# Steps of an attention and Fourier kernel moved between engines and steps: folds, exponentials and the guard of the softmax sums

## The chip, the cores and the metric

The kernel runs on one core of a Trainium2 chip. The metric is the device time of one launch in microseconds, lower is better. A core has five engines that each run their own instructions in order and wait for one another by semaphores: TensorE (PE in the profile; PEld is its weight load), VectorE (DVE), ScalarE (ACT), GpSimd (POOL) and SyncE (SP, which here only issues transfers).

## What is computed

```python
# attention, B=4, H=8, S=768, D=64: 4 sink keys and a window of 128
scores = scale * q @ k.T                       # masked to sink keys and window
a = exp(scores - max(scores))
a = a / (sum(a) + 1e-9)                        # 1e-9: the guard
x = (a @ v)                                    # -> (4, 768, 512)
# Fourier mix and feed-forward
u = x + real(fft(fft(x, axis=1), axis=2))
un = (u - mean(u)) / sqrt(var(u) + 1e-6)
out = u + maximum(un @ w_ch1, 0) @ w_ch2       # 512 -> 2048 -> 512
```

## The kernel before

The four batches are done one after the other, each in six blocks of 128 query rows, 24 blocks in all. A block goes in four steps, one for each pair of heads; `s` counts steps and `k = s % 4`. In every step the program writes out, by the table `SCHEDULE`, what ScalarE ("A"), VectorE ("V"), GpSimd ("G") and TensorE ("T") do, in that order; `SCHEDULE[0]` holds for the first 36 steps (nine blocks), `SCHEDULE[1]` after them. Up to step 97 this order is kept as written; then a scheduler takes over.

The attention of a pair of heads: TensorE makes the scores `s` in PSUM (L702), of which two pairs fit. VectorE merges two key blocks (`merge`, L708) and adds mask and minimum (`soft1`, L720), which frees the scores' place. ScalarE takes the exponentials and their sums (`expo`, L726, two steps later). TensorE turns them (`trans_p`, L751), ScalarE copies the result from PSUM (`copy_p`, tile `pta`, L758), GpSimd cuts it in two by the window (`newer_p` L767, `older_p` L775), and TensorE multiplies by v (`av`, tile `xt`, L789). The four sink keys go their own way: `sink_p` on GpSimd (tile `sk`, L737 and L738), `trans_sink` on TensorE (L809), `copy_sink` on ScalarE (tile `skt`, L814). The turned sink keys lie in the scores' own place of the block two later, so that block's `merge` of its second pair waits for `skt`. Then `copy_x` (L794), `turn_x` and, on VectorE, `store_x` (L819), which multiplies by the inverse of the sums that `inverse` made (L742 adds the guard, L743 takes the reciprocal).

When four blocks of a batch are there, `fourier` sets the batch's Fourier steps in the events "A", "V", "G", "T" and 0 to 3 of later steps, `ready` counting from there. A fold of two blocks (j = 0, 1, 2, four steps apart) is: `fold_n` for the sum on VectorE and the difference on GpSimd (L351), `fold_m` on VectorE (L361) and on GpSimd (L358), `fold_hi` on ScalarE (tile `gh`, L364), `fold_lo` on VectorE (tile `gl`, L367). The middle row of the sequence has its own steps: `put_row`, `mid_sum` (L371) and `mid_row` (tile `sph`: a cast of 33 x 257 at L375, a subtraction of one row at L377). Stage 1 (tiles `za`, `zb`, `zr`, L394) and stage 2 (L421, L442) run on TensorE in the "T" places, and GpSimd adds their results to the blocks (`update`, L458 and L459). The feed-forward network of the first group begins when the attention ends, and overlaps the last batch's Fourier steps and the conversion of the weights (tile `cv`, L590 to L592, on VectorE).

## Time and profile before

| | us |
|---|---|
| median of 3 runs | 787.84 (786.68 to 789.1) |
| the profiled execution, time | 786.78 |
| its span, first to last instruction | 784.9 |
| TensorE busy | 755.2 (96%) |
| VectorE busy | 460.6 (59%) |
| ScalarE busy | 239.0 (30%) |
| GpSimd busy | 177.6 (23%) |

The time of the profiled execution is 1.9 us more than its span: what lies before the first and after the last instruction. Busy shares are over the whole span; the attention takes about the first 220 us of it, and after 262 us TensorE alone is nearly always busy. So the rows below are by stretches of time.

### The profile page before, as it was taken

Reading aid. Unit: us, or ns where it says so; the run is one execution under the profiler, and the core shown is the slowest. Engines: PE = TensorE matmul, PEld = TensorE weight load, DVE = VectorE, ACT = ScalarE, POOL = GpSimd, SP = SyncE. Lnnn points to the kernel's source line nnn. Section 1 sums busy time; section 2 is a strip of 40 time slices with the busy share of each in tenths; the row PEclk is TensorE's granted clock in tenths of the full one; section 3 lists DMA queues with packets and bytes.
Section 4 is the critical chain, followed back from the end, with each engine's and each line's share of the span. In section 5 each row is a group of like instructions: output and inputs, shape, how many; then the busy total and the mean of one; then the engine's idle time right before and its main releaser. Section 6 shows DMA issues by size and latency. Waiting matters only on the chain.

```text
span 784.9 us, 11953 instructions
## 1 busy us (share of the span) xinstructions
PE 755.2 (96%) x4379; PEld 615.8 (78%) x4379; DVE 460.6 (59%) x1354; ACT 239.0 (30%) x704; POOL 177.6 (23%) x283
## 2 busy tenths in 40 slices
PE   7999998988899999999999999999999999999996
PEld 5666876866778878899888888888888888888895
DVE  6788687999999589561356424662456425611211
ACT  4887765756633133221111111111111110110110
POOL 2566477476645255200000000000000000000000
PEclk9999999999999999999999999999999999999999
DMA  9853525433305366120100002000200001000100
GB/s 311 251 171 109 140 84 176 127 112 99 131 27 159 111 196 210 62 71 1 54 1 0 1 9 99 1 1 0 81 1 0 1 0 54 1 1 0 55 1 32
DMA packets 41812, 57.69 MB, mean 74 GB/s; under 512 B 2796, under 2 KB 27500, under 8 KB 41360
## 3 DMA queue, kind: packets, MB, share of 16 engines
q1 hardware_dynamic: 41456, 53.07, 21.7%
q0 software_dynamic: 288, 3.76, 1.2%
q8 instruction: 37, 0.61, 0.3%
q14 instruction: 31, 0.25, 0.1%
HBM read 47.37 MB, written 9.45 MB: 72 GB/s over the span
## 4 chain that ended last, share of the span: by engine, by line
PE 80%; DVE 13%; issue 2%; POOL 1%; ACT 1%; DMA 1%; SPq 0%; DVEq 0%; ACTq 0%; POOLq 0%
PE h L619 33%; PE o L1124 33%; PE xt L789 3%; PE s L702 3%; DVE sm L720 2%; PE pt L751 2%; DVE cv L591 1%; PE za L394 1%; DVE s L708 1%; DVE cv L590 1%; PE a L421 1%; DVE cv L592 1%; DVE f L351 1%; PE x L801 1%; DMA vt<-in_v_sink_dram 1%
## 5 line engine op out<-in xcount | busy, mean ns | idle before, releaser
L1124 PE MATMUL o<-w,h 128*128 128x512 f32 x876 | 216.5, 394 | 0.0
L1117 DVE SCALAR_TENSOR_TENSOR h<-h,h 128x512 fp32r<-128x512 f32 (+1 forms) x107 | 65.4, 611 | 247.7 <-ACT h L1112 247.5
L1124 PEld LDWEIGHTS o<-w,h 128*128 128x128 f32 x876 | 162.8, 188 | 35.5
L1112 ACT ACTIVATE h<-h 128x512 fp32r<-128x512 f32 (+1 forms) x107 | 57.2, 535 | 366.4 <-PE h L619 360.1
L619 PE MATMUL h<-un_slots,w 128*128 128x512 f32 (+1 forms) x576 | 124.7, 365 | 0.0
L619 PEld LDWEIGHTS h<-un_slots,w 128*128 128x128 f32 x576 | 99.6, 188 | 19.6
L619 PE MATMUL h<-un_last,w 128*128 128x512 f32 (+1 forms) x432 | 89.0, 355 | 0.0
L619 PEld LDWEIGHTS h<-un_last,w 128*128 128x128 f32 x432 | 72.7, 188 | 12.8
L726 ACT ACTIVATE sm<-sm,mx 128x132 f32<-128x132 f32 x192 | 75.8, 400 | 7.1 <-DVE mx L720 7.1
L1148 DVE STREAM_TRANSPOSE unf<-un 32x128 f32<-32x128 f32 x224 | 67.7, 302 | 3.2
L702 PE MATMUL s<-ring,q 64*128 64x260 f32 x320 | 51.2, 422 | 12.2 <-DVE mx L720 6.4
L720 DVE CUSTOM_DVE_ANT_0 sm<-s,mask 128x132 f32<-128x132 f32 x192 | 48.7, 292 | 9.3 <-ACT skt L814 2.7
L702 PEld LDWEIGHTS s<-ring,q 64*128 64x128 f32 x320 | 27.1, 188 | 28.2 <-issue 12.4
L608 POOL TENSOR_TENSOR w<-cv,w 128x512 fp32r<-128x512 f32 x25 | 33.9, 1354 | 35.5 <-ACT w L607 35.4
L789 PE MATMUL xt<-ptl,ldv 128*64 128x128 f32 x384 | 38.9, 288 | 0.0
L708 DVE COPY_PREDICATED s<-older,s 128x256 f32<-128x256 uint8 x80 | 33.6, 420 | 7.2 <-ACT skt L814 6.8
L726 ACT ACTIVATION_READ_ACCUMULATOR sm<-sm,mx 128x1 f32 x192 | 36.8, 192 | 0.0
L1124 PE MATMUL o<-w_ring,h 128*128 128x512 f32 x144 | 35.6, 393 | 0.0
L767 POOL TENSOR_SCALAR_AFFINE_SELECT ptl<-pta 128x512 f32<-128x512 f32 x48 | 32.2, 672 | 14.4 <-ACT pta L758 14.4
L789 PEld LDWEIGHTS xt<-ptl,ldv 128*64 128x64 f32 x384 | 21.6, 137 | 14.9 <-issue 8.1
L789 PE MATMUL xt<-pta,ldv 128*64 128x128 f32 x320 | 31.7, 277 | 0.2 <-POOL pta L775 0.2
L751 PE MATMUL pt<-ident,sm 128*128 128x128 f32 x192 | 31.6, 288 | 0.0
(200 smaller groups left out, 1040.9 us busy)
## 6 DMA issues: line engine op xcount, KB each, us to landing
raw<-in_moe_w_ch_dram SPq DMA_DIRECT2D x32, 512.0 KB, 3.7
ldv<-in_v_dram SPq DMA_DIRECT2D x28, 256.0 KB, 3.6
ring<-in_qk_dram SPq DMA_DIRECT2D x24, 264.0 KB, 4.6
out_dram<-u SPq DMA_DIRECT2D x24, 256.0 KB, 3.8
q<-in_qk_dram SPq DMA_DIRECT2D x20, 256.0 KB, 4.2
cst<-in_dft_dram POOLq DMA_DIRECT2D x1, 3348.0 KB, 11.7
ud<-us SPq DMA_DIRECT2D x12, 256.0 KB, 2.2
u<-ud SPq DMA_DIRECT2D x2, 1024.0 KB, 5.1
```

What stands on the lines that cost most here:

```text
L608: G.tensor_tensor(d[1], tf, f32(d[0]), op=ALU.subtract)
L619: T.matmul(ps[:, :tb], a[:, cs], x[:, :, cc, :], start=n == 0, stop=n == 3 * NCC - 1)
L702: T.matmul(ps[:, j, :P + W], st["q", g][rows, hp, :], keys(g, 2 * hp + j), start=True, stop=True)
L708: V.copy_predicated(ps[:, :, P + NS:P + W], older[qi > 2], ps[:, :, 0:P])
L720: V.tensor_tensor_reduce(sm[:, h % 4], ps[:, j, P:P + W], mask[min(qi, 3)], -SCALE, 3.0e38, ALU.add, ALU.min, accum_out=mx[:, 0, h:h + 1])
L726: A.activation(sm[:, h % 4], sm[:, h % 4], AF.Exp, bias=mx[:, 0, h:h + 1], scale=-1.0, accum_out=mx[:, 1, h:h + 1])
L751: T.transpose(ps[:, j], sm[:, j, NS:], ident)
L789: T.matmul(ps[D * j:D * j + D, p, :], st["v", kb(g) - i][:, h, :], a[:, h % 4, :], start=i == 0, stop=i == n - 1)
L1112: A.activation(h[0], ps[:, :tb], AF.Relu)
L1117: V.scalar_tensor_tensor(h[1], ps[:, :tb], 0.0, f32(h[0]), op0=ALU.max, op1=ALU.subtract)
L1124: T.matmul(po[i], a[:, ts_], x, start=f == 0 and n == 0, stop=f == NF - 1 and n == 2)
L1148: V.transpose(unf[32 * q:32 * q + 32, :, r], un[r].rearrange("p (c q j) -> p c q j", c=NCC, q=4)[:, :, q])
```

## The change

Three things are edited. The steps of a fold get other places: `F_STEPS[1]` for j = 0 and 1, `F_STEPS[0]` for the last j and the last batch; GpSimd's `fold_n` comes one step later, its `fold_m`, `fold_hi` and `fold_lo` one step later where j is 0 or 1. The middle row's cast goes from VectorE to ScalarE (`mid_hi`), and its subtraction (`mid_lo`) three steps later. The adding of the guard goes from VectorE to GpSimd as a step of its own (`floor`), and the reciprocal one step later. In ScalarE's lists the exponentials come ahead of the copies in two of the four steps of `SCHEDULE[0]` and one of `SCHEDULE[1]`.

```diff
-F_N, F_M, F_S, ROW = (3, 3), (4, 5), (6, 7), (5, 8, 10)
+F_STEPS = ((3, 4), (4, 5), (6, 7)), ((3, 4), (4, 6), (7, 8))
+ROW = 5, 8, 9, 13
...
-    "inverse": 7,
+    "floor": 6,
+    "inverse": 8,
...
         "A": [
             ["copy_x", "copy_p", "copy_sink", "expo", "A", "sink_hi"],
-            ["copy_x", "copy_sink", "expo", "sink_hi", "A", "copy_p"],
+            ["copy_x", "expo", "copy_sink", "copy_p", "A", "sink_hi"],
             ["copy_x", "copy_p", "copy_sink", "expo", "A", "sink_hi"],
-            ["copy_x", "A", "copy_p", "copy_sink", "expo", "sink_hi"],
+            ["expo", "copy_x", "A", "copy_p", "copy_sink", "sink_hi"],
...
-            ["copy_x", "copy_sink", "A", "sink_hi", "copy_p", "expo"],
+            ["copy_x", "expo", "copy_sink", "copy_p", "A", "sink_hi"],
...
         "G": [
...
-            ["newer_p", "older_p", "sink_p", "G"],
+            ["newer_p", "older_p", "sink_p", "floor", "G"],
...
-                def mid_row():
+                def mid_hi():
+                    A.copy(sph[:NR, :257], t_["x0"][:, :257])
+
+                def mid_lo():
                     t = t_["x0"]
-                    V.tensor_copy(sph[:NR, :257], t[:, :257])
                     lo = sph[NR - 1:NR, :257]
                     V.tensor_tensor(lo, t[NR - 1:NR, :257], f32(lo), op=ALU.subtract)
...
+                    f_n, f_m, f_s = F_STEPS[0 if tail or j == NHALF - 1 else 1]
...
-                at(ready[0] + ROW[2], "V", mid_row)
+                at(ready[0] + ROW[2], "A", mid_hi)
+                at(ready[0] + ROW[3], "V", mid_lo)
...
                     def inverse(g):
                         mx = st["mx", g]
-                        V.tensor_scalar_add(mx[:, 2], mx[:, 1], 1e-9)
                         V.reciprocal(mx[:, 2], mx[:, 2])
+
+                    def floor(g):
+                        mx = st["mx", g]
+                        G.tensor_scalar_add(mx[:, 2], mx[:, 1], 1e-9)
```

What stands where, in the program's order. Line numbers of the change are some lines higher. First VectorE in the second batch, between the last `soft1` of a block (its accumulator is the first row) and the first `merge` of the next, where the fold j = 2 begins. Before:

```order
L720 ISA mx_1658 128x1
L742 TENSOR_SCALAR mx_1512<-mx_1512 128x8
L743 RECIPROCAL mx_1512<-mx_1512 128x8
L375 CAST sph<-xr_1440 33x257
L377 TENSOR_TENSOR sph<-xr_1440,sph 1x257
L367 TENSOR_TENSOR gl_1429<-f_1_1_1654,gh_1428 128x512
L351 TENSOR_TENSOR f_1_2_1778<-us_2_1072,us_5_1075 128x512
L708 COPY_PREDICATED s_0_1769<-older_122,s_0_1769 128x2x128
```

And with the change, the same place and the one two merges later:

```order
L727 ISA mx_1657 128x1
L749 RECIPROCAL mx_1512<-mx_1512 128x8
L354 TENSOR_TENSOR f_1_2_1776<-us_2_1069,us_5_1072 128x512
L715 COPY_PREDICATED s_0_1766<-older_122,s_0_1766 128x2x128
...
L727 ISA mx_1780 128x1
L370 TENSOR_TENSOR gl_1429<-f_1_1_1653,gh_1428 128x512
L364 TENSOR_TENSOR f_1_2_1776<-f_1_2_1776 128x255
L829 TENSOR_TENSOR u_65<-x_1801,mx_1385 128x512
L382 TENSOR_TENSOR sph<-xr_1440,sph 1x257
L715 COPY_PREDICATED s_2_1825<-older_122,s_2_1825 128x2x128
```

Of six instructions between two pairs' scores two are left; `gl` and the subtraction for `sph` now stand two pairs later, and the guard and the cast have left VectorE.

Second GpSimd in the same batch, from the cut of one block (`ptl_1`) to that of the next pair (`ptl_3`). Before:

```order
L767 AFFINE_SELECT ptl_1_1730<-pta_1_1694 128x512
L775 AFFINE_SELECT pta_1_1694<-pta_1_1694 128x512
L358 TENSOR_TENSOR f_1_1_1654<-f_1_1_1663 128x255
L737 CAST sk_1761<-sm_0_1657 128x2x16
L738 TENSOR_TENSOR sk_1761<-sm_0_1657,sk_1761 128x2x16
L458 TENSOR_TENSOR u_64<-u_64,d_1_1650 128x257
L459 TENSOR_TENSOR u_64<-u_64,d_1_1650 128x255
L767 AFFINE_SELECT ptl_3_1785<-pta_3_1751 128x512
L351 TENSOR_TENSOR f_1_2_1787<-us_2_1072,us_5_1075 128x512
L775 AFFINE_SELECT pta_3_1751<-pta_3_1751 128x512
```

And with the change:

```order
L777 AFFINE_SELECT ptl_1_1731<-pta_1_1691 128x512
L785 AFFINE_SELECT pta_1_1691<-pta_1_1691 128x512
L753 TENSOR_SCALAR mx_1512<-mx_1512 128x8
L744 CAST sk_1757<-sm_0_1656 128x2x16
L745 TENSOR_TENSOR sk_1757<-sm_0_1656,sk_1757 128x2x16
L463 TENSOR_TENSOR u_64<-u_64,d_1_1650 128x257
L464 TENSOR_TENSOR u_64<-u_64,d_1_1650 128x255
L361 TENSOR_TENSOR f_1_1_1653<-f_1_1_1704 128x255
L777 AFFINE_SELECT ptl_3_1783<-pta_3_1752 128x512
L785 AFFINE_SELECT pta_3_1752<-pta_3_1752 128x512
```

The guard is new behind the cut; GpSimd's half of `fold_m`, which completes the tile that `gh` is cast from, now stands behind `sk` and an update; and its half of `fold_n` no longer stands between the two cuts of a pair.

Third ScalarE around the same cast `gh`. Before:

```order
L758 COPY pta_3_1751<-pt_3_1738 128x512
L364 CAST gh_1428<-f_1_1_1654 128x512
L726 ACTIVATE sm_2_1727,mx_1658<-sm_2_1727,mx_1658 128x132 x2
L814 CAST skt_1811<-s_1_1772 128x128
L758 COPY pta_1_1813<-pt_1_1799 128x512
L726 ACTIVATE sm_2_1727,mx_1658<-sm_2_1727,mx_1658 128x132 x2
```

And with the change:

```order
L768 COPY pta_3_1752<-pt_3_1739 128x512
L367 CAST gh_1428<-f_1_1_1653 128x512
L733 ACTIVATE sm_2_1728,mx_1657<-sm_2_1728,mx_1657 128x132 x4
L824 CAST skt_1809<-s_1_1769 128x128
L768 COPY pta_1_1811<-pt_1_1795 128x512
```

The cast `gh` stands at the same place; the exponentials of the block's last pair have moved from behind `pta` to ahead of `skt`, and both now follow `gh`.

## Rows read from the trace of the kernel before

**Rows 1.** Windows: length, busy of PE, PEld, DVE, ACT, POOL; PEclk, DMA.
```profile
48.00:70.00 22.00, 19.96 (x178) 13.27 (x178) 20.30 (x86) 18.16 (x70) 16.80 (x32) 1.00 0.33 97
70.00:98.00 28.00, 28.00 (x259) 23.30 (x257) 17.90 (x78) 19.14 (x71) 12.53 (x26) 1.00 0.52 147
98.00:125.00 27.00, 23.01 (x193) 17.49 (x189) 23.06 (x81) 15.98 (x60) 20.95 (x37) 0.94 0.22 61
140.00:186.00 46.00, 39.70 (x357) 30.39 (x358) 44.63 (x164) 28.90 (x103) 30.22 (x52) 1.00 0.35 103
200.00:262.00 62.00, 56.91 (x350) 48.38 (x347) 58.72 (x100) 24.08 (x56) 34.05 (x31) 0.97 0.34 107
```

**Rows 2.** Timeline of VectorE: start, duration, line, operation.
```profile
115.00 0.65 DVE L375 CAST sph<-xr 33x257 fp32r<-33x257 f32 x1
115.69 0.74 DVE L377 TENSOR_TENSOR sph<-xr,sph 1x257 fp32r<-1x257 f32 x1
116.46 1.01 DVE L367 TENSOR_TENSOR gl<-f,gh 128x512 fp32r<-128x512 f32 x1
117.39 1.76 DVE L351 TENSOR_TENSOR f<-us,us 128x512 f32<-128x512 f32 x1
```

**Rows 3.** Timeline of TensorE, the wait in brackets.
```profile
120.19 0.71 PE L702 MATMUL s<-ring,q 64*128 64x260 f32 x4 [2.31 <-DVE mx L720]
```

**Rows 4.** Windows of 4 us where TensorE's clock was lower, columns as rows 1.
```profile
121.00:125.00 4.00, 3.92 (x26) 2.72 (x26) 2.88 (x14) 1.23 (x5) 3.77 (x9) 0.57 0.02 1
210.00:214.00 4.00, 4.00 (x18) 3.58 (x16) 4.00 (x9) 1.53 (x3) 1.66 (x2) 0.57 0.53 170
```

**Rows 5.** Windows of line L742 alone, the guard: busy and count.
```profile
48.00:70.00 22.00, 0.83 (x4) 1.00 0.33 97
98.00:125.00 27.00, 1.11 (x3) 0.94 0.22 61
140.00:186.00 46.00, 1.11 (x5) 1.00 0.35 103
200.00:262.00 62.00, 1.08 (x2) 0.97 0.34 107
```

**Rows 6.** Windows of line L375 alone, the cast of the middle row.
```profile
48.00:70.00 22.00, 0.23 (x1) 1.00 0.33 97
98.00:125.00 27.00, 0.65 (x1) 0.94 0.22 61
140.00:186.00 46.00, 0.56 (x1) 1.00 0.35 103
200.00:262.00 62.00, 0.72 (x1) 0.97 0.34 107
```

**Rows 7.** Line L737, GpSimd's small cast: count, ns minimum/median/maximum.
```profile
L737 POOL CAST sk<-sm x48: 205/212/500, 10.6 to 206.1; 128x32 fp32r<-128x32 f32 x48
```

**Rows 8.** Timeline of GpSimd beside rows 2.
```profile
113.61 0.73 POOL L358 TENSOR_TENSOR f<-f 128x255 f32<-128x255 f32 x1
...
114.78 0.73 POOL L458 TENSOR_TENSOR u<-u,d 128x257 f32<-128x257 f32 x1
115.46 0.69 POOL L459 TENSOR_TENSOR u<-u,d 128x255 f32<-128x255 f32 x1
...
116.90 1.70 POOL L351 TENSOR_TENSOR f<-us,us 128x512 f32<-128x512 f32 x1
```

**Rows 9.** Timeline of ScalarE beside rows 2.
```profile
114.37 0.62 ACT L364 CAST gh<-f 128x512 fp32r<-128x512 f32 x1
...
117.25 0.27 ACT L814 CAST skt<-s 128x128 fp32r<-128x128 f32 x1 [1.47 <-PE s L809]
```

**Rows 10.** Waits, 0 to 225 us: total, times, longest.
```profile
ACT skt L814 <- PE s L809: 24.4, 18, 2.7
...
DVE s L708 <- ACT skt L814: 6.8, 11, 1.3
```

**Rows 11.** Line L726, an exponential: count, ns minimum/median/maximum.
```profile
L726 ACT ACTIVATE sm<-sm,mx x192: 387/399/427, 5.9 to 205.5; 128x132 f32<-128x132 f32 x192
```

**Rows 12.** Line L351, the fold's first step: ns minimum/median/maximum by form.
```profile
L351 DVE TENSOR_TENSOR f<-us,us x9: 639/693/1758, 95.8 to 228.6; 128x512 f32<-128x512 f32 x9
```

More of the change, by code (lines that the diff above doesn't have):

```diff
@@ L99 @@
             ["newer_p", "older_p", "G", "sink_p"],
-            ["newer_p", "G", "sink_p", "older_p"],
+            ["newer_p", "G", "sink_p", "older_p", "floor"],
             ["newer_p", "older_p", "sink_p", "G"],
@@ L466, in fourier @@
                     k = ready[j]
+                    f_n, f_m, f_s = F_STEPS[0 if tail or j == NHALF - 1 else 1]
                     e0, e1 = FOLD_TAIL if tail else FOLD_ENG
                     eng = {"V": V, "G": G}
-                    at(k + F_N[0], e0, lambda j=j: fold_n(eng[e0], j, 0))
-                    at(k + F_N[1], e1, lambda j=j: fold_n(eng[e1], j, 1))
-                    at(k + F_M[0], e0, lambda j=j: fold_m(eng[e0], j, 0))
-                    at(k + F_M[1], e1, lambda j=j: fold_m(eng[e1], j, 1))
-                    at(k + F_S[0], "A", lambda j=j: fold_hi(j))
-                    at(k + F_S[1], "V", lambda j=j: fold_lo(j))
+                    at(k + f_n[0], e0, lambda j=j: fold_n(eng[e0], j, 0))
+                    at(k + f_n[1], e1, lambda j=j: fold_n(eng[e1], j, 1))
+                    at(k + f_m[0], e0, lambda j=j: fold_m(eng[e0], j, 0))
+                    at(k + f_m[1], e1, lambda j=j: fold_m(eng[e1], j, 1))
+                    at(k + f_s[0], "A", lambda j=j: fold_hi(j))
+                    at(k + f_s[1], "V", lambda j=j: fold_lo(j))
                 at(ready[0] + ROW[0], "V", put_row)
                 at(ready[0] + ROW[1], "V", mid_sum)
-                at(ready[0] + ROW[2], "V", mid_row)
+                at(ready[0] + ROW[2], "A", mid_hi)
+                at(ready[0] + ROW[3], "V", mid_lo)
                 k = ready[2] + S1
@@ L951, in window_attention @@
                             "newer_p": newer_p, "older_p": older_p, "av": av, "copy_x": copy_x, "copy_sink": copy_sink,
-                            "trans_sink": trans_sink, "turn_x": turn_x, "inverse": inverse, "store_x": store_x,
+                            "trans_sink": trans_sink, "turn_x": turn_x, "inverse": inverse, "floor": floor, "store_x": store_x,
                             "sink_hi": lambda g: g and g % NB == 0 and sink_hi(g // NB), "sink_lo": lambda g: g and g % NB == 0 and sink_lo(g // NB),
```

## The prediction

> **What bounds the kernel now.** I read the windows by stretch first, since the busy shares of the whole span mix two kernels: behind 262 us TensorE is never short of work and the change touches nothing there. Before that the stretches are of two kinds [rows 1]. From 70 to 98 us TensorE is busy for all 28.00 us, and whatever VectorE saves there buys nothing (125 to 140 and 186 to 200 us are of this kind too). Where the folds of a batch lie, TensorE waits: 22.00 - 19.96 = 2.04 us from 48 to 70, 3.99 us from 98 to 125, 6.30 us from 140 to 186, and 5.09 us from 200 to 262. In these four VectorE is busy for 20.30 of 22, 23.06 of 27, 44.63 of 46 and 58.72 of 62 us. So 17.4 us of TensorE's waiting are all that this change can win directly, and VectorE is what it has to win them from.
>
> Then I read VectorE's timeline at the longest of these waits, in the second batch. Four instructions of the fold stand in a row between two pairs of scores: the middle row's cast, its subtraction, `gl`, and the sum of the next fold, from 115.00 to about 119.1 us [rows 2]. The scores that TensorE has to make next lie behind them, and it waits 2.31 us, released by VectorE [rows 3]. After that wait its granted clock is 0.57 on average for 4 us, which is the lower level of 1.2 GHz for most of them [rows 4]. A second window like it stands at 210 us.
>
> **The change, part by part.** The guard leaves VectorE 24 times. Only those in the four stretches count: 0.83, 1.11, 1.11 and 1.08 us of busy time, 14 instructions in all [rows 5]. From the end of one such instruction to the next some 0.03 us pass (the same that separates 115.69 + 0.74 from 116.46 in [rows 2]), so 14 x 0.03 = 0.4 us come on top. One of the four in the first stretch stands ahead of a VectorE wait, so I take off 0.2 us. That makes 4.13 + 0.4 - 0.2 = 4.3 us.
>
> The cast of the middle row leaves VectorE four times, once in each stretch: 0.23 + 0.65 + 0.56 + 0.72 = 2.16 us [rows 6], with 0.03 us each 2.3 us.
>
> By stretch the two make 1.0, 1.9, 1.85 and 1.9 us, each well below TensorE's waiting there, so I count all of it: 6.6 us.
>
> The steps that move (`gl`, the fold's first sum, the subtraction of the row, GpSimd's halves) are the same instructions as before. Their total is credited with nothing. What the move can give is in where they stand: the row of four in [rows 2] becomes one, and `gl` and the subtraction come two pairs later, beside `fold_m` and `store_x`. The wait of 2.31 us should then break into shorter ones, and shorter waits have not brought the clock down: the whole of 140 to 186 us, with 6.30 us of waits, was granted 1.00 [rows 1]. The drop at 121 us cost (1 - 0.57) x 4 = 1.7 us of TensorE's work [rows 4]; VectorE was busy for 2.88 of those 4 us, so 1.1 us of it was time in which VectorE, too, had nothing to do. I credit 1.1 us, with bounds of 0 (the wait only moves) and 3.4 us (both drops go, at their full 1.7 us). The one at 210 us stands in the scheduler's part, where the order of the conversions changes in ways that I can't price; I leave it in.
>
> Now what is added. GpSimd's guard has no row. The nearest is its cast of a 128 x 32 tile, 205 ns at least, 212 in the median and 500 at most [rows 7]; a tile of 128 x 8 is smaller, so 0.2 us, 24 x 0.2 = 4.8 us of GpSimd's time. It stands behind the second cut of the block's first half, and the reciprocal comes two steps later. GpSimd is free for 5.2 of 22, 6.05 of 27 and 15.8 of 46 us in the fold stretches [rows 1], so nobody should wait for the result. What can cost is that the two engines disturb each other: the fold's sum took 1.76 us where GpSimd's own half (116.90, 1.70 us long) was running [rows 2, 8], against 639 ns at least [rows 12]. VectorE's instruction ended 0.5 to 0.6 us after GpSimd's, as if it had begun only then. So the bounds for 24 more GpSimd instructions are 0 and 24 x 0.2 = 4.8 us, and since most of VectorE's instructions here (merges, soft1) read PSUM and show no such rows, I take a tenth, 0.5 us. A gain is possible as well, since the cast no longer runs on VectorE; it is within this.
>
> The Trainium skill's page "SBUF — State Buffer" (section "Who interferes with whom") says it as a rule: a VectorE instruction with two SBUF inputs and a GpSimd instruction that reads SBUF take the shared read port as a whole, and whichever comes second stands still. The rows agree (0.64 against 1.76 us). By that rule the guard on GpSimd is a new holder of the port and speaks against the change, up to the 4.8 us of the bound, and the fold's halves may meet anew in their new places; that is the second rival below.
>
> ScalarE's order. In the steady blocks an exponential pair takes 2 x 0.39 us [rows 11] and moves into time in which ScalarE waited anyway: 24.4 us over 18 waits for the sink keys' transposition, 1.36 us each [rows 10]. I price it at 0; without that cover it would hold `skt` back by up to 0.78 us a block, and VectorE already waits 6.8 us for `skt` [rows 10].
>
> One wait is added. `gh` needs GpSimd's half of `fold_m`, which before stood ahead of the sink cast (113.61) and now stands behind it and behind an update of 0.73 + 0.69 us [rows 8]. `gh` itself stays at its place behind `pta`, at 114.37 in the old trace [rows 9]. Three folds have an update in front in this way (both early ones of the second batch and one of the third, by the order). Behind a late `gh` stand both exponential pairs of the block's second half and `skt`, and behind `skt` VectorE's merge. GpSimd's work in front is 1.42 us longer, ScalarE had 1.47 us of slack ahead of `skt` there [rows 9], and the merge is itself to come earlier by what VectorE saves. Bounds 0 and 3 x 1.42 = 4.3 us; I take half, 2.1 us. The middle row's cast on ScalarE is at most the 0.62 us of `gh` [rows 9], four times, and lies in the same waits: 0.
>
> **The sum.** 4.3 + 2.3 + 1.1 - 0.5 - 2.1 = 5.1 us. 786.78 - 5.1 = 781.7 us for an execution like the profiled one. The median of the runs is 1.06 us above that execution, so I forecast 782.8 us (-0.65%).
>
> **Rivals.**
> 1. *More than the sum.* If the row of four was the cause of most of TensorE's waits in the stretches, half of the 17.4 us go and both clock drops with them: 8.7 + 3.4 = 12 us, 775.8. For it: VectorE's contended instructions stand in that row (1.01 and 1.76 us [rows 2]). Against it: VectorE is busy 85 to 97% of these stretches [rows 1], and what moves is not removed.
> 2. *Given back by the port.* `gl` and `fold_m` now stand where GpSimd does its half of `fold_n`. A fold's instruction that meets it grows by 1.76 - 0.64 = 1.1 us [rows 2, 12]. With the six early folds of three batches meeting it at half that more than before, 3.4 us are lost, and with 0.5 of the sum's other costs doubled the gain is about 1.2 us: 786.6, no change. For it: GpSimd is busy 76 to 78% of the first two stretches [rows 1]. Against it: before, GpSimd's half met the same engine's sum just as often.
> 3. *Slower: ScalarE stands still at `gh`.* In the three places the exponentials, `skt` and the next merge all queue behind it. If `gh` is late by 1.9 us (1.42 and a sink cast of 0.5), VectorE and then TensorE wait as long, and a wait of about 2 us brings TensorE's clock down for another 1.7 us [rows 3, 4]. 3 x (1.9 + 1.7) = 10.8 us against the 7.2 us of the sum without its 2.1: 3.6 us slower, 791.4. It decides where the late `gh` exceeds ScalarE's slack ahead of `skt`, 1.47 us [rows 9], by more than VectorE comes earlier. Against it: the merge has no wait in that place in the old trace.
>
> The change does what it says by the order, so that it does nothing is no rival of its own; that VectorE's savings end in TensorE-bound time is part of rival 2's outcome.
>
> **How the numbers follow.** Chances: the sum 0.55, rival 1 0.10, rival 2 0.21, rival 3 0.14. The forecast's own range is 778 to 786. 0.3% of 787.84 is 2.4 us, about what a measurement of this kernel can tell from no change, so faster is below 785.5 and slower above 790.2. Faster takes rival 1 and nearly all of the sum, 0.64; same takes rival 2 and the sum's upper end, 0.23; slower is 0.13. The range leaves out the far half of rival 1 and most of rival 3: 777 to 789.
>
> **What would show it.** Right: line L742's successor stands on GpSimd at 0.1 to 0.3 us; VectorE's busy time falls by at least 6 us (4.1 of guard in the four stretches and 2.2 of cast, more or less by contention); TensorE's waits in the four stretches fall by about 5 us, above all in 98 to 125 us; no 2 us wait near 120 us, and the clock there is 1.00. Wrong: ScalarE idle ahead of `gh` until GpSimd's `fold_m` for over 1 us, with VectorE waiting for `skt` behind it (rival 3); VectorE's `gl` at 1.0 us or more beside GpSimd's `fold_n` (rival 2); VectorE waiting for GpSimd ahead of the reciprocal, which I exclude. The forecast would also be wrong if the order of the conversions behind step 97 moves TensorE's waits after 200 us by more than 2 us either way.

## The result: 0.27% slower, and the profile after

The changed kernel takes 789.07 us in the median of 20 runs (787.37 to 793.2), the kernel before beside it 787.14 us (785.75 to 789.1). The ratio is 1.0027 with a 95% interval of 1.0016 to 1.0037. So it is 2 us slower where I forecast 5 us faster. The profiled execution took 788.54 us, its span is 786.8 us.

The first view is the windows by stretch, against [rows 1]: length, then busy time of PE, PEld, DVE, ACT, POOL, then the granted clock. The last row, 44 to 262 us, holds all folds; ahead of it the guard and ScalarE's new order act as well.

```profile
48.00:70.00 22.00, 20.03 (x172) 13.60 (x170) 17.32 (x74) 16.83 (x65) 17.45 (x31) 0.92 0.31 86
70.00:98.00 28.00, 26.44 (x238) 21.51 (x236) 17.28 (x74) 18.18 (x66) 12.81 (x29) 1.00 0.51 147
98.00:125.00 27.00, 23.90 (x220) 18.61 (x218) 19.48 (x80) 18.05 (x69) 19.92 (x34) 1.00 0.25 70
140.00:186.00 46.00, 40.55 (x356) 32.04 (x354) 40.56 (x165) 30.45 (x111) 30.95 (x56) 1.00 0.39 114
200.00:262.00 62.00, 56.27 (x363) 48.44 (x362) 59.52 (x106) 26.24 (x64) 38.53 (x35) 1.00 0.35 115
44.00:262.00 218.00, 198.60 (x1610) 159.18 (x1609) 180.03 (x588) 130.31 (x451) 142.22 (x227) 0.98 0.39 120
```

The same stretch, 44 to 262 us, in the kernel before:

```profile
44.00:262.00 218.00, 200.42 (x1600) 159.93 (x1601) 190.68 (x607) 129.66 (x446) 132.10 (x210) 0.98 0.39 119
```

VectorE is lighter by more than I said: 17.32 in place of 20.30 us, 19.48 in place of 23.06, 40.56 in place of 44.63 (but 59.52 in place of 58.72 in the last stretch). From 44 to 262 us it is busy for 180.0 us, before for 190.7. Yet TensorE's idle time there went up, from 218 - 200.42 = 17.6 to 218 - 198.60 = 19.4 us. The next view shows VectorE's waits from 44 to 262 us (total, times, longest).

```profile
DVE s L715 <- ACT skt L824: 14.7, 13, 2.5
DVE sm L727 <- ACT skt L824: 3.2, 2, 1.9
```

In the same stretch of the kernel before:

```profile
DVE s L708 <- ACT skt L814: 3.9, 7, 1.3
DVE sm L720 <- ACT skt L814: 2.7, 2, 1.6
```

VectorE waits 17.9 us for `skt`, before it was 6.6 us. So over the whole change a longer wait for `skt` stands against the 10.7 us that were taken off VectorE. The experiments below show that the two don't come from the same parts.

The first batch's fold is the best place to see where the time goes. First VectorE's timeline (start, duration, line, operation, the wait in brackets). L370 is `gl` (before L367), L364 `fold_m`, L374 the middle row's sum, L829 `store_x`, L715 a merge.

```profile
58.18 0.43 DVE L715 COPY_PREDICATED s<-older,s 128x256 f32<-128x256 uint8 x1 [0.78 <-ACT skt L824]
...
59.08 1.08 DVE L370 TENSOR_TENSOR gl<-f,gh 128x512 fp32r<-128x512 f32 x1
60.08 0.85 DVE L364 TENSOR_TENSOR f<-f 128x255 f32<-128x255 f32 x1
60.85 0.41 DVE L374 TENSOR_TENSOR xr<-xr 33x255 f32<-33x255 f32 x1
61.19 0.67 DVE L829 TENSOR_TENSOR u<-x,mx 128x512 f32<-128x512 f32 x1
61.79 0.41 DVE L715 COPY_PREDICATED s<-older,s 128x256 f32<-128x256 uint8 x1
...
67.76 0.43 DVE L715 COPY_PREDICATED s<-older,s 128x256 f32<-128x256 uint8 x1 [2.54 <-ACT skt L824]
```

The row of four of [rows 2] is gone, and another row of four stands here, 2.7 us long, between the second and the third pair of scores. Beside it, ScalarE's timeline: L377 is the middle row's cast, L367 `gh`.

```profile
61.29 0.41 ACT L377 CAST sph<-xr 33x257 fp32r<-33x257 f32 x1 [1.60 <-DVE xr L374]
...
63.81 0.62 ACT L367 CAST gh<-f 128x512 fp32r<-128x512 f32 x1 [0.38 <-POOL f L361]
...
120.57 0.62 ACT L367 CAST gh<-f 128x512 fp32r<-128x512 f32 x1 [2.16 <-POOL f L361]
```

The cast waits for the row's sum, with a pair of exponentials right behind it, and at 120.57 `gh` waits 2.16 us for GpSimd, as rival 3 has it. TensorE's timeline shows the price of the row (eight score matmuls in one line), and the windows below it the clock. The profile names no releaser for this wait ("issue"); that the row sets it follows from the times, since the pair's `soft1` behind the merge of 61.79 us ends at 62.74 us.

```profile
62.85 2.18 PE L709 MATMUL s<-ring,q 64*128 64x260 f32 x8 [1.66 <-issue]
```

```profile
61.00:65.00 4.00, 2.34 (x12) 0.94 (x10) 3.90 (x18) 3.33 (x11) 2.32 (x6) 0.76 0.52 133
65.00:69.00 4.00, 3.85 (x33) 3.05 (x33) 1.43 (x9) 2.53 (x13) 2.81 (x6) 0.82 0.00 0
184.00:188.00 4.00, 2.49 (x14) 1.48 (x16) 4.00 (x15) 2.75 (x11) 3.93 (x6) 0.74 0.39 128
188.00:192.00 4.00, 4.00 (x33) 3.59 (x30) 2.56 (x12) 1.53 (x6) 2.46 (x5) 0.83 0.50 170
```

The low clock of [rows 4], at 121 and 210 us, is gone: both windows are at 1.00 in this execution. Two others have come, near 64 and 187 us, and they cost the same: (0.24 + 0.18) x 4 = 1.7 us, and 1.7 us again.

### The profile page after: what moved, and what is told of

Its sections match the earlier page's. It is cut to its first block, busy times and chain, and to the rows that moved or that the text cites. A ratio compares the mean times of both kernels' runs of the same rounds, so it can differ in the third digit from the quotient of the medians.

```text
span 786.8 us, 11950 instructions
## 1 busy us (share of the span) xinstructions
PE 754.0 (96%) x4379; PEld 616.1 (78%) x4379; DVE 450.2 (57%) x1326; ACT 239.7 (30%) x708; POOL 189.6 (24%) x307
## 4 chain that ended last, share of the span: by engine, by line
PE 78%; DVE 13%; DMA 3%; issue 3%; ACT 2%; POOL 1%; SPq 0%; DVEq 0%; ACTq 0%; POOLq 0%
PE o L1134 32%; PE h L626 32%; PE xt L799 3%; PE s L709 3%; DMA ring<-in_qk_dram 3%; DVE cv L598 2%; PE pt L761 2%; DVE sm L727 1%; PE za L399 1%; ACT sm L733 1%; DVE s L715 1%; DVE cv L597 1%; DVE cv L599 1%; PE a L426 1%; PE x L811 1%
## 5 line engine op out<-in xcount | busy, mean ns | idle before, releaser
L615 POOL TENSOR_TENSOR w<-cv,w 128x512 fp32r<-128x512 f32 x25 | 36.7, 1469 | 33.9 <-ACT w L614 33.7
L715 DVE COPY_PREDICATED s<-older,s 128x256 f32<-128x256 uint8 x80 | 33.8, 422 | 18.7 <-ACT skt L824 17.5
L777 POOL TENSOR_SCALAR_AFFINE_SELECT ptl<-pta 128x512 f32<-128x512 f32 x48 | 33.8, 705 | 32.6 <-ACT pta L768 30.2
L768 ACT COPY pta<-pt 128x512 f32<-128x512 f32 x48 | 28.1, 585 | 10.4 <-PE pt L761 10.2
```

The source lines that it names most:

```text
L615: G.tensor_tensor(d[1], tf, f32(d[0]), op=ALU.subtract)
L715: V.copy_predicated(ps[:, :, P + NS:P + W], older[qi > 2], ps[:, :, 0:P])
L777: G.affine_select(lo, a, [[0, 4], [s, P]], compare_op=ALU.is_ge, fill=0.0, base=0, channel_multiplier=-s)
```

## The experiments

Eighteen kernels were timed, each against the kernel before on the same chip. Three theories stood at first: ScalarE stands still at its two late casts (A), VectorE and GpSimd get in each other's way (B), and, after the first runs, VectorE's pile has only moved (C). The table lists all results; behind the ratio stand four readings of each profile. *Idle* is 218 us less TensorE's busy time from 44 to 262 us, *clock* the sum of (1 - granted clock) x 4 us over the windows of 4 us from 40 to 264 us, *VectorE* its busy time and *skt* its wait for `skt`, both from 44 to 262 us. These four are of the profiled execution alone, which need not be like the median one: e9's took 788.36 us with a median of 784.76, e17's 787.03 with 785.30, e10's 783.31 with 785.00.

| kernel | ratio to before (95%) | idle | clock | VectorE | skt |
|---|---|---|---|---|---|
| before | 1 | 17.6 | 3.4 | 190.7 | 6.6 |
| after | 1.0027 (1.0016 to 1.0037) | 19.4 | 3.4 | 180.0 | 17.9 |
| e1 row's cast at 10 | 1.0051 (1.0039 to 1.0063) | 19.2 | 5.2 | 180.5 | 15.7 |
| e2 GpSimd's `fold_m` at 5 | 1.0061 (1.0044 to 1.0078) | 18.5 | 6.8 | 178.6 | 16.8 |
| e3 both | 1.0059 (1.0039 to 1.0080) | 20.8 | 3.4 | 181.1 | 16.6 |
| e4 old fold steps | 1.0006 (0.9990 to 1.0022) | 17.4 | 1.7 | 185.4 | 10.5 |
| e5 `gl` at 10 | 0.9974 (0.9964 to 0.9984) | 16.2 | 3.4 | 182.4 | 11.1 |
| e6 guard alone | 0.9968 (0.9958 to 0.9978) | 17.4 | 0.0 | 185.6 | 6.5 |
| e7 cast alone | 0.9966 (0.9954 to 0.9978) | 16.3 | 1.7 | 188.6 | 7.0 |
| e8 order alone | 1.0055 (1.0042 to 1.0068) | 19.4 | 3.4 | 192.3 | 7.1 |
| e9 old order, `gl` at 10 | 0.9972 (0.9963 to 0.9980) | 17.8 | 6.8 | 179.9 | 13.7 |
| e10 guard and cast | 0.9975 (0.9963 to 0.9987) | 17.8 | 0.0 | 184.5 | 7.8 |
| e11 old order | 1.0001 (0.9991 to 1.0010) | 19.2 | 5.2 | 180.1 | 13.4 |
| e12 order, GpSimd's sum at 4 | 1.0074 (1.0061 to 1.0087) | 17.8 | 5.1 | 189.5 | 7.7 |
| e13 guard twice | 1.0041 (1.0019 to 1.0063) | 20.1 | 3.4 | 193.8 | 7.2 |
| e14 fold behind first pair | 0.9995 (0.9978 to 1.0012) | 19.0 | 1.7 | 183.2 | 8.0 |
| e15 order, third pair | 1.0032 (1.0018 to 1.0046) | 20.1 | 1.7 | 193.0 | 6.4 |
| e16 order, first pair | 1.0036 (1.0023 to 1.0049) | 18.5 | 3.4 | 190.6 | 8.6 |
| e17 guard and cast, cast at 10 | 0.9967 (0.9954 to 0.9980) | 18.4 | 3.4 | 184.8 | 7.8 |
| e18 guard, cast, late order | 0.9986 (0.9971 to 1.0001) | 17.3 | 0.0 | 185.0 | 8.1 |

The mean granted clock of every execution was measured too, and it varies within one kernel: from 0.987 to 0.997 in the 113 executions of the kernel before, from 0.992 to 0.998 in the eleven of e10. An estimate of what the clock costs, at the most, is (1 - clock) x span; it is too high where TensorE waits at the low clock. Its mean is 5.2 us in the 29 executions of the kernel before that ran beside e10 and e11, 3.2 us in e10 and 6.0 us in e11; 5.8 us in e8 with 5.6 us beside it; 8.5 us in e13 with 4.9 us beside it.

### Are ScalarE's late casts the cause?

These four are edits of the changed kernel. e1:

```diff
-ROW = 5, 8, 9, 13
+ROW = 5, 8, 10, 13
```

> The changed kernel with one number different: ScalarE's cast of the middle row one step later (10 in place of 9), behind the next pair of exponentials. Theory A (ScalarE stands still at the two casts that wait): the cast waited 1.60 us at 61.3, 1.05 at 116.3, 2.10 at 171.6 and 1.05 at 225.9 for VectorE's sum of that row, with exponentials behind it; these waits fall below 0.3 us each, the exponentials and the sink cast come earlier, and of the 2.9 us that the first batch's folds lost about 1.5 come back, of the third batch about 1: 2 to 3 us less than the changed kernel, 786 to 787, ratio to the kernel before 0.999 to 1.000. Theory B (the cost is contention of VectorE with GpSimd at gl and the fold's sums): the same instructions stand in the same order on VectorE, so nothing is won, ratio 1.002 to 1.004.

e2, and e3 with both this edit and that of e1:

```diff
-F_STEPS = ((3, 4), (4, 5), (6, 7)), ((3, 4), (4, 6), (7, 8))
+F_STEPS = ((3, 4), (4, 5), (6, 7)), ((3, 4), (4, 5), (7, 8))
```

> The changed kernel with GpSimd's half of fold_m of the first two folds back at step 5 (as before the change; all else as changed). Theory A: gh waited for it 2.16 us at 120.6 and 0.92 at 127.9; at step 5 it stands in front of the sink cast and of the update, in a time where GpSimd was idle for 1.5 us, gh begins at once behind pta, and VectorE's wait of 2.09 us for skt at 122.9 goes: 1.5 to 2.5 us less than the changed kernel, about 787, ratio 0.999 to 1.001. Theory B: fold_m on GpSimd moves away from VectorE's next fold sum (1.23 us in place of 0.72), half a microsecond per fold at most, at most 1 us: 1.001 to 1.003.

> The changed kernel with both edits: the middle row's cast at step 10, and GpSimd's half of fold_m at step 5. Theory A: the two gains stand in different steps and add, 3.5 to 5.5 us less than the changed kernel: 783.5 to 785.5, ratio 0.995 to 0.998, which is about what the prediction's sum without its term for the late gh comes to (5.1 + 2.1 = 7.2 us less than before), less the loss near 33 us. Theory B: at most 1 us less than the changed kernel, ratio 1.001 to 1.003.

e4:

```diff
-F_STEPS = ((3, 4), (4, 5), (6, 7)), ((3, 4), (4, 6), (7, 8))
+F_STEPS = ((3, 3), (4, 5), (6, 7)), ((3, 3), (4, 5), (6, 7))
```

> The changed kernel with the fold's steps of before on all engines (first sums at 3, fold_m at 4 and 5, gh at 6, gl at 7); guard, row's cast and ScalarE's order stay as changed. Theory A: gl no longer stands in front of fold_m and of the row's sum, so the cast at step 9 waits 1.0 us less than in the changed kernel, and gh waits no more for GpSimd; the row of four is then one of three on VectorE, since the row's cast is gone from it, and a wait of TensorE of 1 to 1.5 us is back near 120 us: in all 1 to 3 us less than the changed kernel, 786 to 788, ratio 0.999 to 1.001. Theory B: the old places of the fold had less contention: 3 us or more less than the changed kernel, ratio below 0.998.

Theory A fell. In e1 the cast waits for VectorE's sum 0.9 us once, in place of 5.8 us in four places; in e2 `gh` waits for GpSimd 0.8 us once, in place of 3.7 us in four; in e3 both are short. None became faster, all three are slower than the changed kernel. VectorE's timeline in e1 shows why taking the wait away won nothing.

```profile
59.75 0.69 DVE L370 TENSOR_TENSOR gl<-f,gh 128x512 fp32r<-128x512 f32 x1
60.36 0.85 DVE L364 TENSOR_TENSOR f<-f 128x255 f32<-128x255 f32 x1
61.13 0.84 DVE L374 TENSOR_TENSOR xr<-xr 33x255 f32<-33x255 f32 x1
61.90 0.68 DVE L829 TENSOR_TENSOR u<-x,mx 128x512 f32<-128x512 f32 x1
62.50 0.41 DVE L715 COPY_PREDICATED s<-older,s 128x256 f32<-128x256 uint8 x1
```

TensorE's timeline in e1, at the same place:

```profile
63.57 0.71 PE L709 MATMUL s<-ring,q 64*128 64x260 f32 x4 [1.66 <-issue]
```

The row of four is still there, the merge behind it comes at 62.50, and TensorE waits the same 1.66 us. With the old fold steps (e4) that row has no `gl` in it, VectorE waits 10.5 us for `skt` and not 17.9, and 1.0006 against 1.0027 brings back 1.7 us (the intervals overlap). That e1 to e3 are slower than the changed kernel and not equal to it goes for e1 and e2 with the clock column, for e3 with the idle one; which wait brings the clock down I could not foresee in any of them.

### One part at a time

e5 is the changed kernel with `gl` in the other gap; e6 to e8 are the kernel before with one part each (the fold's steps alone were not run).

e5:

```diff
-F_STEPS = ((3, 4), (4, 5), (6, 7)), ((3, 4), (4, 6), (7, 8))
+F_STEPS = ((3, 4), (4, 5), (6, 7)), ((3, 4), (4, 6), (7, 10))
```

> The changed kernel with gl of the first two folds at step 10 in place of 8, so that it stands behind the reciprocal, in the other of VectorE's two gaps between pairs of scores. The two earlier theories were the waits of ScalarE (A) and contention (B); the waits could be taken away without a gain. Theory C (the pile moved): the change put gl in front of fold_m, the row's sum and store_x, a new row of four of 2.7 to 3.1 us between two pairs of scores (59.75 to 62.50 with the row's cast late), while the other gap holds 0.9 us and VectorE then waits 1.1 to 2.5 us for skt. With gl there the gaps are 2.0 and 1.6 us, TensorE's waits of 1.8 and 1.5 us near 63 and 72 us fall below 1.0 each, VectorE's wait for skt falls by half from its 13 us, and the time is 1.5 to 3 us below the changed kernel: 786 to 787.5, ratio 0.998 to 1.001. Theory A: gh and the row's cast wait as before this edit, 789, ratio 1.002 to 1.004. Theory B: gl meets GpSimd's first sum of the next fold less or more, within 1 us of the changed kernel, 1.001 to 1.004.

e6, with `floor` as in the change:

```diff
-    "inverse": 7,
+    "floor": 6,
+    "inverse": 8,
...
-                        V.tensor_scalar_add(mx[:, 2], mx[:, 1], 1e-9)
```

> The kernel before with one part of the change alone: the guard on GpSimd behind the second cut, and the reciprocal a step later; the rest as before. The prediction's terms: -4.3 + 0.5, 3.8 us less than before, ratio 0.995. Theory C: the guard takes 0.2 us out of one of the two gaps, but which pair TensorE waits for is decided by the longer gap and by skt, so most of it turns into VectorE's wait for skt (6.8 us in the kernel before): 0 to 1.5 us less, ratio 0.998 to 1.000. Theory B: the guard disturbs VectorE by up to 4.8 us: 1.000 to 1.006.

e7, with the steps 9 and 13:

```diff
-                    V.tensor_copy(sph[:NR, :257], t[:, :257])
+                    A.copy(sph[:NR, :257], t_["x0"][:, :257])
```

> The kernel before with the row's cast alone on ScalarE (step 9) and its subtraction at step 13. The prediction's terms: -2.3 us, and the part of the clock drop at 121 us that hung on the row of four (-1.1): ratio 0.996 to 0.997. Theory C: the gap with gl, the row's cast and its subtraction is the longer one in the kernel before (2.3 us against 1.8 near 60 us), so that taking cast and subtraction out of it is worth more than the guard: 1 to 3 us less, and the wait of 2.31 us near 120 us falls below 1.5, ratio 0.996 to 0.999. Theory A: the cast waits for the row's sum and holds ScalarE up by about 1 us in each of four batches: 1.001 to 1.004.

e8, which takes the new "A" rows of the change and nothing else (here the first of them):

```diff
-            ["copy_x", "copy_sink", "expo", "sink_hi", "A", "copy_p"],
+            ["copy_x", "expo", "copy_sink", "copy_p", "A", "sink_hi"],
...
```

> The kernel before with ScalarE's new order alone (exponentials ahead of the copies that wait). The prediction: 0 us, ratio 1.000. From the traces: the second cut on GpSimd then begins at the moment at which VectorE makes two small products near 33.4 us, which grew from 0.21 and 0.26 to 0.62 and 0.69 us, once, 0.8 us in all; theory C expects no more than that, ratio 1.000 to 1.002. If the order were what holds skt back in each block (0.39 to 0.78 us a block, as the prediction bounded it), 24 blocks would cost 5 us and more: ratio above 1.005.

In VectorE's timeline of e5 the row is one of three (and TensorE's wait behind it 1.11 us):

```profile
60.10 0.76 DVE L364 TENSOR_TENSOR f<-f 128x255 f32<-128x255 f32 x1
60.79 0.84 DVE L374 TENSOR_TENSOR xr<-xr 33x255 f32<-33x255 f32 x1
61.56 0.67 DVE L829 TENSOR_TENSOR u<-x,mx 128x512 f32<-128x512 f32 x1
...
64.04 0.69 DVE L370 TENSOR_TENSOR gl<-f,gh 128x512 fp32r<-128x512 f32 x1
```

One number, `gl` from step 8 to 10, is worth 1.0027 - 0.9974 = 0.0053, 4.2 us. That is theory C in kind and more than its range, though TensorE's wait fell to 1.11 us and not below 1.0. With ScalarE's old order the same number is worth 2.3 us (e9 below against e11).

Guard and cast alone give 2.5 and 2.7 us. For the cast that is within the prediction's range and theory C's; for the guard it lies between the prediction's 3.8 us and theory C's 1.5 at the most. In e6 TensorE's idle time falls from 12.5 to 10.3 us between 44 and 200 us, as the prediction has it, and rises from 5.1 to 7.1 us from 200 to 262 us, most of which the scheduler orders. One of the waits there is for GpSimd's second cut: it is 1.4 us or more in every kernel with the guard on GpSimd, and 0.2 us or none in the others. TensorE's waits from 200 to 262 us, in the kernel before and the changed one:

```profile
PE xt L789 <- POOL pta L775: 0.2, 1, 0.2
PE xt L799 <- POOL pta L785: 1.5, 2, 1.1
```

With the guard the scheduler also orders GpSimd's other work anew there, so what the guard itself does to this wait isn't told apart.

ScalarE's order, which I had priced at nothing, costs 4.3 us alone. That is the total expected if it held `skt` back in every block, but VectorE's wait for `skt` is 7.1 us, against 6.6 before. VectorE's timeline in e8, at the second fold of the first batch (`gl` and the fold's sum):

```profile
56.90 1.02 DVE L369 TENSOR_TENSOR gl<-f,gh 128x512 fp32r<-128x512 f32 x1
57.84 1.76 DVE L353 TENSOR_TENSOR f<-u 128x512 f32<-128x512 f32 x1
```

GpSimd's timeline there, its half of the same fold:

```profile
57.35 1.71 POOL L353 TENSOR_TENSOR f<-u 128x512 f32<-128x512 f32 x1
```

TensorE's timeline behind it:

```profile
60.65 0.71 PE L705 MATMUL s<-ring,q 64*128 64x260 f32 x4 [1.20 <-DVE mx L723]
```

In the kernel before these two are 0.69 us each, since GpSimd's half begins behind them:

```profile
55.18 0.69 DVE L367 TENSOR_TENSOR gl<-f,gh 128x512 fp32r<-128x512 f32 x1
55.79 0.69 DVE L351 TENSOR_TENSOR f<-u 128x512 f32<-128x512 f32 x1
57.58 1.27 POOL L351 TENSOR_TENSOR f<-u 128x512 f32<-128x512 f32 x1
```

With the exponentials of the third pair ahead of the copies, GpSimd gets its sink cast earlier, has it behind it earlier, and begins its half of the fold (1.71 us) beside VectorE's. VectorE's two grow by 1.4 us in all, and TensorE waits 1.20 us behind them.

### Do the parts add?

e9 is e5 with the "A" rows of before, which undoes the edit of e8; e10 is the kernel before with the edits of e6 and e7; e11 is the changed kernel with the "A" rows of before.

> The changed kernel with ScalarE's order of before, and gl of the first two folds at step 10; guard, row's cast and the fold's other steps stay as changed. If the parts add as they were measured alone (guard -2.5 us, row's cast -2.7, order +4.3, gl at step 10 in place of 8 -4.2), this is 4.3 us below the kernel with gl at step 10: 781, ratio 0.991 to 0.993, and the fastest here. If VectorE is no longer what TensorE waits for once guard and cast are gone, the parts don't add: 783 to 785, ratio 0.995 to 0.998.

> The kernel before with the guard on GpSimd and the row's cast on ScalarE, no moved steps and no new order. The prediction's two terms for them came to 6.6 us less 0.5; measured alone they gave 2.5 and 2.7. If they add: 5.2 us less than before, 782, ratio 0.993 to 0.994. If they save the same waits twice: 784 to 785, ratio 0.996 to 0.997.

> The changed kernel with ScalarE's order of before and nothing else different. If the order's cost of 4.3 us, measured alone, stands in the changed kernel as well: 4.3 us below the changed kernel, 784.8, ratio 0.996 to 0.999. If the moved steps had already taken the fold out of GpSimd's way, so that the order costs only its 1.5 us ahead of 48 us: 787.5, ratio 1.000 to 1.002.

e12, an edit of e8 (the second number is GpSimd's):

```diff
-F_STEPS = ((3, 3), (4, 5), (6, 7)), ((3, 3), (4, 5), (6, 7))
+F_STEPS = ((3, 4), (4, 5), (6, 7)), ((3, 4), (4, 5), (6, 7))
```

> The kernel before with ScalarE's new order, and GpSimd's half of the fold's first sum at step 4 in place of 3, behind the second cut. Theory B in its new form (earlier exponentials let GpSimd begin its half of the fold earlier, just when VectorE makes gl and its own half: gl 1.02 us and the fold's sum 1.76 us at 57 us, against 0.69 and 0.69 before): with GpSimd's half a step later gl and VectorE's half are back to 0.6 to 0.8 us each, the waits of TensorE of 1.36 us at 60.6 and 1.89 at 69.5 fall below 1.0, and about 2 of the order's 4.3 us come back, ratio 1.001 to 1.004. If the order costs its time by holding skt behind the exponentials: no change, ratio 1.004 to 1.007.

e10, e11 and the changed kernel are one chain, a part more at each step: guard and cast 0.9975 (-2.0 us), with the moved steps 1.0001 (+2.0), with ScalarE's order 1.0027 (+2.0). They don't add to what each gives alone: guard and cast together are worth no more than one of them, the order costs 2.0 us in the changed kernel and 4.3 alone, and with `gl` at 10 it costs nothing (0.9974 with it, 0.9972 without). By the other way, over e4, the order costs 2.4 us and the moved steps 1.7.

By the estimate from all executions, the clock gives 2.0 us with guard and cast and takes 2.7 us with the moved steps, about what the times differ by; with the order alone (e8) it changes by 0.2 us.

e11 came out as the second of its expectations, an order that costs its time ahead of 48 us. The windows from 22 to 48 us, in the kernel before and the changed one:

```profile
22.00:48.00 26.00, 25.72 (x264) 18.85 (x262) 20.07 (x107) 21.47 (x86) 14.68 (x34) 1.00 0.79 233
22.00:48.00 26.00, 24.56 (x252) 18.21 (x252) 19.62 (x99) 21.18 (x86) 15.28 (x37) 1.00 0.78 235
```

TensorE's idle time there is 0.28 us before, in e10 and in e11, and 1.44 us in the changed kernel. Behind 44 us it is the same with the order and without (19.4 and 19.2 us), although VectorE's wait for `skt` grows from 13.4 to 17.9 us.

e12 held in its place and failed in the total. At the second fold VectorE's two instructions are back to 0.64 and 1.12 us and the wait there to 0.69 us. At the third fold the middle row's two, 0.67 and 1.37 us beside GpSimd, stay long, and TensorE waits 1.80 us at 68.28, with a mean clock of 0.64 from 68 to 72 us.

### What was open: VectorE's limit, and the order's two rows

e13, an edit of the kernel before:

```diff
                         V.tensor_scalar_add(mx[:, 2], mx[:, 1], 1e-9)
+                        V.tensor_scalar_add(mx[:, 2], mx[:, 1], 1e-9)
                         V.reciprocal(mx[:, 2], mx[:, 2])
```

> The kernel before with VectorE's guard written twice in each block (the second writes the same values), so 24 instructions of 0.17 us and 0.03 us of spacing more on VectorE, 14 of them in the four fold stretches. If VectorE bounds these stretches as the prediction held: 14 x 0.31 = 4.3 us slower by the same sum, ratio 1.004 to 1.006. If the loop of scores and skt sets TensorE's waits: TensorE's idle time from 44 to 262 us (17.6 us before) moves by less than 1.5 us, and the time follows the clock drops (two of 1.7 us before): ratio 0.998 to 1.003.

e14, an edit of e10 (the row for the later blocks likewise, and `other_masks` at step 4 stays ahead of the scores):

```diff
-            ["inverse", "store_x", "sink_lo", "V", 3, 0, 1, 2, "merge", "soft1"],
+            ["inverse", "store_x", "sink_lo", 3, 0, 1, 2, "merge", "soft1", "V"],
```

> Guard on GpSimd and row's cast on ScalarE (the earlier run at 0.9975), and VectorE's fold instructions of the step of a block's first pair (the fold's first sum and gl) put behind that pair's scores in place of ahead of them, where VectorE waits for skt of the block before; the conversions and normalizing steps that go by the same list move with them. If the place and not the amount of VectorE's work sets TensorE's waits: VectorE's wait for skt (6 to 8 us) falls below 4, the row between the block's second and first pair shrinks from 1.6 to 2.3 us to below 1, TensorE's idle time from 44 to 262 us falls by 2 to 5 us, and the ratio is 0.990 to 0.995, faster than all others here. If skt itself is what TensorE waits for: within 1 us of the kernel without this edit, 0.996 to 0.999.

e15, an edit of the kernel before:

```diff
-            ["copy_x", "A", "copy_p", "copy_sink", "expo", "sink_hi"],
+            ["expo", "copy_x", "A", "copy_p", "copy_sink", "sink_hi"],
```

> The kernel before with one row of ScalarE's new order, in the first nine blocks: the exponentials of step 3 ahead of the copy of the attention's output, of gh and of the second cut's copy. If these let GpSimd finish its sink cast earlier and begin its half of the fold beside VectorE's gl and sum: gl at 1.0 us and the sum at 1.2 to 1.8 us near 57 us, batch 0 loses 1.5 to 2.5 us between 50 and 72 us, nothing is lost ahead of 44 us: ratio 1.002 to 1.004. If not: 1.000.

e16, an edit of the kernel before:

```diff
-            ["copy_x", "copy_sink", "expo", "sink_hi", "A", "copy_p"],
+            ["copy_x", "expo", "copy_sink", "copy_p", "A", "sink_hi"],
```

> The kernel before with the other row of ScalarE's new order, in the first nine blocks: the exponentials of step 1 ahead of skt and of the first cut's copy. If this row only moves GpSimd's cut beside the two small products near 33.4 us and a copy near 21 us: 1.3 to 1.5 us lost ahead of 44 us and nothing behind it, ratio 1.001 to 1.003. If the exponentials hold skt back in every block: 0.4 us and more in each of 9 blocks, 3.6 us, ratio 1.004 to 1.006.

e13 speaks for VectorE as the bound: 3.2 us more of busy time (4.3 were expected) cost 3.2 us, of which 2.5 us show as idle time of TensorE in its profile (17.6 to 20.1 us). By the mean clock of its seven executions up to 3.5 us may be the clock, so the split isn't settled. Going the other way, e10 takes 6.2 us off VectorE and leaves TensorE's idle time as it was (17.8 us); its wait for `skt` grows by 1.2 us only, and with the moved steps (e11) by 5.6 us more. So more work on VectorE cost its full time and less work wasn't worth its own; which wait takes over in e10 is open.

e14 refutes the simple form of theory C, that VectorE's fold only has to stand where VectorE waits for `skt`: its wait stays at 8.0 us, and the kernel is 1.6 us slower than e10, which neither expectation has. The test isn't clean, since conversions and normalizing moved with the list.

Both rows of the order cost time, 2.5 us (e15) and 2.8 us (e16) alone, 4.3 together. VectorE's timeline of e15 shows a collision at the third fold, at the middle row's cast (at the second, where it was expected, `gl` took 0.64 us and the sum 1.12):

```profile
66.08 1.20 DVE L375 CAST sph<-xr 33x257 fp32r<-33x257 f32 x1
```

GpSimd's timeline beside it, its half of the fold's first sum:

```profile
65.86 1.27 POOL L351 TENSOR_TENSOR f<-u 128x512 f32<-128x512 f32 x1
```

That cast took 0.23 us before:

```profile
62.21 0.23 DVE L375 CAST sph<-xr 33x257 fp32r<-33x257 f32 x1
```

Ahead of 48 us, where nothing was to be lost, e15's profile has 2.36 us of TensorE's idle time, 2.25 of them in one wait for a transfer at 24.43 us; why it waits there is open. In e16 `gl` and the sum near 58 us are 0.64 and 0.68 us, undisturbed; its loss lies in part ahead of 44 us, at two small products of the first token, which the changed kernel shows too. VectorE's timeline of the changed kernel:

```profile
33.42 0.62 DVE L936 TENSOR_SCALAR scratch<-scratch 32x4 f32<-32x4 f32 x1
34.08 0.69 DVE L937 TENSOR_SCALAR scratch<-scratch 32x64 f32<-32x64 f32 x1
```

GpSimd's timeline beside them, the two cuts:

```profile
33.40 0.63 POOL L777 TENSOR_SCALAR_AFFINE_SELECT ptl<-pta 128x512 f32<-128x512 f32 x1 [0.50 <-ACT pta L768]
34.10 0.64 POOL L785 TENSOR_SCALAR_AFFINE_SELECT pta<-pta 128x512 f32<-128x512 f32 x1
```

Each ends with the cut beside it. Before they stood between two cuts:

```profile
33.18 0.21 DVE L926 TENSOR_SCALAR scratch<-scratch 32x4 f32<-32x4 f32 x1
33.43 0.26 DVE L927 TENSOR_SCALAR scratch<-scratch 32x64 f32<-32x64 f32 x1
```

The difference is 0.8 us, once.

e17 is e10 with the edit of e1. e18 is e10 with the new "A" rows in the second half of the table (`SCHEDULE[1]`, from step 36 on) alone.

> Guard on GpSimd and row's cast on ScalarE (the run at 0.9975, steps and order of before), and the cast one step later, 10 in place of 9, where it doesn't wait for the row's sum. If ScalarE's standing still there reaches TensorE: 1 to 2 us less than without the edit, ratio 0.994 to 0.9965. If, as with the moved steps, the wait lies beside others: 0.9965 to 0.999.

> Guard on GpSimd, row's cast on ScalarE, and ScalarE's new order in the blocks from the tenth on only; fold steps of before. If the order costs only in the first nine blocks: as guard and cast without it, ratio 0.996 to 0.999. If it holds skt back in the later blocks too, about half of the 2.4 us that it cost beside guard and cast: 0.9985 to 1.001.

e17 differs from e10 by less than the intervals: the cast's wait costs nothing measurable there either. e18 is inconclusive, its interval holds both expectations.

## Why the prediction was wrong, step by step

- **VectorE is what TensorE waits for, "so I count all of it: 6.6 us".** This step failed. The durations were right: 24 guards on GpSimd at 0.24 us (the estimate was 0.2), and VectorE 10.7 us lighter, 6.2 of it by these two parts (e10). Alone the terms are near what they gave, 2.5 us of 3.8 for the guard and 2.7 of 2.3 for the cast. Together they gave 2.0 of 6.1. I had read VectorE's busy share of 85 to 97% as room for every saved microsecond; but with both parts TensorE's idle time from 44 to 262 us didn't fall (17.6 us before, 17.8 in e10), and the 2.0 us are those of the clock, by the estimate from all executions. The wait for `skt` [rows 10] rose to 17.9 us in the change, but only to 7.8 us by these two parts, so it isn't shown to be what took over; that stays open.
- **The moved steps, "credited with nothing", with 1.1 us of clock.** This step failed too. The row of four at 115 us went, and in the profile of the change so did the low clock behind it; in e11, with the same steps, the clock is 0.72 and 0.85 from 124 to 132 us, so that was luck. But "beside `fold_m` and `store_x`", where the text itself put `gl`, is a row of four of 2.7 us (2.0 in e11). That "shorter waits have not brought the clock down" didn't hold either: it fell behind the 1.66 us at 62.85 us. The step cost 2.0 us (e10 to e11) in place of giving 1.1, by the estimate from all executions through the clock. `gl` at step 10 takes 4.2 us off, 2.3 with the old order.
- **ScalarE's order, "I price it at 0".** This step failed too: 2.0 us in the change, 4.3 alone. I looked for its cost at `skt`. That wait did grow with it in the change, by 4.5 us, but TensorE's idle time behind 44 us didn't; alone it grew by 0.5 us. What I didn't follow is GpSimd behind ScalarE: the exponentials release its sink cast, so an earlier exponential moves GpSimd's work against VectorE's. Alone this shows at the folds (e8, e15); in the change it shows at the two products at 33.4 us, with 1.2 us more of TensorE's idle time from 22 to 48 us (0.4 of it for a transfer), and in the row with `gl`, 2.0 us long without the order and 2.7 with it. That is the mechanism of rival 2, set off by another part. The Trainium skill's page "SBUF — State Buffer", section "Who interferes with whom", counts VectorE's casts, copies and products with a scalar, where their operands meet certain conditions, among the instructions that can lock GpSimd out or be locked out, beside those with two SBUF inputs, which were all that I had taken from it. The rows agree: the cast went from 0.23 to 1.20 us, the product from 0.21 to 0.62 us.
- **The late `gh`, +2.1.** The wait came as described, 3.7 us over four places, the longest 2.16 us. Its price did not: without it (e2) nothing is faster. Rival 3 named the right side and a mechanism that is seen, but not the one that decides.
- **VectorE waiting ahead of the reciprocal, "which I exclude".** It happened once, 0.5 us, and in e6 four times, 2.1 us. That "nobody should wait for the result" also left out GpSimd's cuts behind the guard, for which TensorE waits 1.5 us after 200 us, against 0.2 before.

So 2 us slower is: guard and cast -2.0, moved steps +2.0, order +2.0. Shown are these three sums, added in this order, the new row with `gl`, and the collisions in their places. The clock's share is an estimate: nearly all of the first two terms and little of the order's. In the profiles its low windows come in portions of 1.7 us and stand in another place in nearly every kernel, between none and four of them; e6 and e10 have none in the profiled execution, but other executions of theirs were granted less (down to 0.992). A rule for which wait brings one wasn't found.

The fastest versions are the row's cast alone (0.9966), guard and cast with the cast at 10 (0.9967) and the guard alone (0.9968), 2.5 to 2.7 us below the kernel before and 4.6 to 4.8 below the change; the runs don't tell them apart, nor from e5, e9 and e10 (0.9972 to 0.9975).

## What to carry to other kernels

An engine that is busy for 90% of a stretch need not be the only bound of it: before every saving on it is counted, look which wait comes next in its own queue, and how much later that one ends. Where differences are of a few microseconds, compare the granted clock of all executions and not of one profile. When an instruction is moved between fixed points (here pairs of scores), add up the row that it lands in, as carefully as the one that it leaves. When an engine with idle time gets a new order, follow what it releases on the other engines and which shared resource they then use at the same time.

## What the runs showed of the hardware that I had not expected

A VectorE instruction of 0.21 us on a 32 x 4 tile took 0.62 us beside a GpSimd cut of 0.63 us and ended with it: so in this place a small one paid the whole length of its neighbour. And the clock: a wait of TensorE of 1.66 us at 62.85 us was followed by a stretch with a mean clock of 0.76 and 0.82 in two windows of 4 us, while in e1 the same 1.66 us at 63.57 us was followed by 1.00. The windows of e1:

```profile
62.00:66.00 4.00, 2.20 (x24) 1.51 (x24) 3.90 (x17) 3.07 (x12) 3.78 (x7) 1.00 0.50 137
66.00:70.00 4.00, 3.85 (x40) 2.57 (x34) 2.84 (x10) 2.30 (x10) 2.76 (x7) 1.00 0.00 0
```

Here the length of a single wait doesn't tell whether the clock falls behind it.
